# Talking-heads attention and a squared-ReLU MLP: the order of a step that has transposes and two A v pairs

## The chip, the cores and the metric

The kernel runs on one core of a Trainium2 chip. The metric is device time in microseconds, from one launch that holds everything; the time before is the median of three runs. Five queues work side by side: TensorE (matmuls and transposes, PE in the rows; its weight loads are PEld), VectorE (DVE), ScalarE (ACT), GpSimd (POOL) and SyncE (SP, which issues most transfers). In each queue the instructions stand in the order in which the program wrote them, and they wait for semaphores of the other queues.

## The reference

The inputs are q, k, v (4 batches, 12 heads, 448 positions, 64 channels), two 12 x 12 matrices that mix heads, and the weights of an MLP (768 to 2048 to 768).

```python
scores = scale * np.matmul(q, k.transpose(0, 1, 3, 2))
scores = np.einsum('bhij,hg->bgij', scores, w_pre)
scores = scores - np.max(scores, axis=-1, keepdims=True)
attn = np.exp(scores)
attn = attn / (np.sum(attn, axis=-1, keepdims=True) + 1e-09)
attn = np.einsum('bhij,hg->bgij', attn, w_post)
attn_out = np.matmul(attn, v)
x = np.ascontiguousarray(attn_out.transpose(0, 2, 1, 3)).reshape(B * S, H * D)
h = x @ w_in
r = np.maximum(h, 0.0)
return (s * (r * r) + b) @ w_out
```

Everything is float32. The kernel keeps that precision by splitting an operand into a high part (rounded) and a low part (what the rounding left) and adding three matmuls per product.

## The kernel before, in words

**Chunks, blocks, steps.** The query rows of each batch are cut into 4 chunks of 110 or 118 rows, 16 in all. A chunk is cut into 11 or 12 blocks of 9 or 10 rows; a block holds its rows for all 12 heads, so up to 120 partitions, by 448 keys. There are 180 blocks, and the attention is one loop of steps (line 851). Step s starts each block at a different stage: it transfers block s+5 out of the chunk's scores (`relayout`, SyncE), splits s+2 into high and low part (`split`, GpSimd), mixes the heads of s (`premix`, three matmuls into `pm`, L603), takes its maximum (VectorE, L605), its exponentials and their sum (ScalarE, L610, and the sum's scaling into `st`, L614, called total(s) below), normalizes s-1 (`normalize`: a reciprocal on VectorE, L622, and the half-precision high part `eh` on ScalarE, L624), forms the remainder of s-1 (VectorE, L631), mixes s-3 again with the second matrix (`postmix`, 12 matmuls into `po`, L646), and copies the result of s-4 into the chunk's tile A (`evacuate`, VectorE, L662).

**What is planned into steps.** Lines 675 to 781 make a list `plan` of work for other chunks, sorted by step and by an order within it: loads (order 0), transposes of q or k (order 1), A v pairs (order 2) and q k pairs (order 3). `prep_q` and `prep_k` transpose with TensorE into a PSUM tile of the tag `sc`, copy the high part to `Tq` or `Tk` on ScalarE (L482, L462) and append the low part to a list `later`; `low_parts` (L239) subtracts on VectorE what stands in that list. `qk_pair` calls `low_parts` and then multiplies two heads (six matmuls, L503) into a tile of the same tag `sc`, which has one buffer, and ScalarE copies them to the scores S (L513). `av_pair` multiplies A with v for two heads (16 matmuls, L531); `copy_x` copies finished sums out (ScalarE, L553).

Lines 715 to 725 take the A v pairs of a chunk two by two. Where not both of their steps follow a step with transposes, both pairs go into one step, and the transposes of the step before that one are moved into it:

```python
                    steps[i] = steps[i + 1] = steps[j]
                    for n, x in enumerate(plan):
                        if x[0] == steps[j] - 1 and x[3] in (prep_q, prep_k):
                            plan[n] = (steps[j], *x[1:])
```

That happens for 20 steps: 15, 20, 26, 45, 49, 56, 60, 65, 71, 90, 94, 101, 105, 110, 116, 135, 139, 146, 150 and 157. In 26, 71 and 116 it is k that is transposed, in the others q. Each of them also has a q k pair.

**The order within a step.** The main loop writes, for one of these steps: an instruction of the weights' conversion (`convert_step`, VectorE, only in some steps), `normalize(s-1)`, `premix(s)` with maximum and exponentials, `evacuate(s-4)`, `remainder(s-1)`, the loads, `postmix(s-3)`, and then the plan: transposes, two A v pairs, the q k pair with the low part ahead of it. So the transposes' high part is on ScalarE behind total(s), and their low part on VectorE behind the remainder.

After the attention come the two GEMMs of the MLP in two rounds over the hidden width (`gemm1_part` L254, `gemm2` L311); the first pieces of the first one are mixed into the last chunk's steps.

Of the kernel before, what the change touches and what calls it, by code (L numbers as in the profile page):

```python
# [21 lines left out]
def talking_heads_attention__then__act_relu2_kernel(  # L22
# [14 lines left out]
    B, H, S, D = q.shape  # L37
# [8 lines left out]
    NP = H // 2  # L46
# [18 lines left out]
    blocks = []  # L65
# [10 lines left out]
    NB = len(blocks)  # L76
# [112 lines left out]
    def convert_step(upto):  # L189

        if done["run"] is None:
            if done["conv"] >= min(upto, len(units)):
                return False
            done["run"] = conversion(done["conv"])
        try:
            next(done["run"])
        except StopIteration:
            done["run"] = None
            done["conv"] += 1
        return True  # L200
# [33 lines left out]
    later = []  # L234
# [7 lines left out]
    turn = {"bank": 0, "ops": 0}  # L242
# [327 lines left out]
        if ci >= NCH - 2:  # L570
            copy_x()

    blk_t, hl_t, po_t, e_t, eh_t = {}, {}, {}, {}, {}

    def relayout(t):
        ci, i0, ni = blocks[t]
# [17 lines left out]
    def premix(t):  # L594
        n = blocks[t][2] * H
        hl = hl_t.pop(t)

        tag = "px" if t % 3 == 2 else "pm"
        pm = ps.tile([P, 512], F32, tag=tag, name=f"pm_{t}", bufs=banks.count(tag))
        for _ in range(2 if t < first[1] - 1 else 1 if t < first[1] + 3 else 0):  # L600
            nc.tensor.matmul(pm, keep[:, :P], keep, start=True, stop=True)
        for m, (w, x) in enumerate(((wpre_lo, 0), (wpre_hi, 1), (wpre_hi, 0))):
            nc.tensor.matmul(pm[:n, :S], w[:n, :n], hl[:n, x, :], start=(m == 0), stop=(m == 2))  # L603
        st = smp.tile([BP, 4], F32, tag="st", name=f"st_{t}")
        nc.vector.tensor_reduce(  # L605
            out=st[:n, 0:1], in_=pm[:n, :S], axis=AX.X, op=ALU.max, negate=True
        )

        e = pm[:, :S]
        nc.scalar.activation(e[:n], e[:n], AF.Exp, bias=st[:n, 0:1], accum_out=pm[:n, S:S + 1])  # L610
        e_t[t] = (e, st)

        total = pm[:, S:S + 1]
        nc.scalar.activation(  # L614
            st[:n, 2:3], total[:n], AF.Copy, scale=2.0 ** -15, bias=1e-9 * 2.0 ** -15
        )

    def normalize(t):

        n = blocks[t][2] * H  # L620
        e, st = e_t[t]
        nc.vector.reciprocal(st[:n, 3:4], st[:n, 2:3])  # L622
        eh = blkp.tile([BP, 2, S], F16, tag="eh", name=f"eh_{t}", bufs=3)
        nc.scalar.activation(eh[:n, 0, :], e[:n], AF.Copy, scale=st[:n, 3:4])  # L624
        eh_t[t] = eh
# [10 lines left out]
    def postmix(t):  # L636
        ci, i0, ni = blocks[t]
        n = ni * H
        eh = eh_t.pop(t)
        if i0 == 0:  # L640
            a_t[ci] = ap_.tile([P, NC, H, CH], F32, tag="A", name=f"A_{ci}")
        po = ps.tile([P, 512], F32, tag="po", name=f"po_{t}", bufs=2)
        for c in range(NC):
            j0 = min(c * P, S - P)
            for m, (x, y) in enumerate(((1, 0), (0, 1), (0, 0))):
                nc.tensor.matmul(  # L646
                    po[:, c * BP:(c + 1) * BP],
                    eh[:n, x, j0:j0 + P],
                    wpost[:n, y].rearrange("p g i -> p (g i)"),
                    start=(m == 0),  # L650
                    stop=(m == 2),
                )
        po_t[t] = po
# [10 lines left out]
    LD, LS = 5, 2  # L664
    CONV0 = 12
# [7 lines left out]
    plan, load = [], {}  # L673

    def at(step, order, f, *args):
        plan.append((step, order, len(plan), f, args))
# [12 lines left out]
    for ci in range(2, NCH):  # L689
        b, _, _ = chunks[ci]  # L690
        w0 = first[ci - 1] - LD
        news = chunks[ci - 1][0] != b
        back = w0 - (first[ci - 2] - LD)
        if news:
            starts = (w0 - back + 6, w0 - back + 2)
        else:
            starts = (w0 - back + (10 if back == 12 else 8), w0 + 4)
        for half, step in enumerate(starts):
            at(step, 1, prep_q, ci, half)
            load[step] = 0.375  # L700
        if ci > 2:
            at(min(starts) - 8, 0, load_q, ci)
        for p, step in enumerate(visits(ci)):
            if news:
                t = w0 - back + 8 if p == 0 else w0 + 2 * p - 2
                at(t, 1, prep_k, b, p)
                load[t] = 0.6
                at(t - 6, 0, load_k, b, p)
            at(step, 3, qk_pair, ci, p)
            load[step] = load.get(step, 0) + QK_COST  # L710
    for ci in range(NCH):
        b = chunks[ci][0]
        w0 = first[ci + 1] + 4
        if ci < NCH - 2:
            after = visits(ci + 3) if ci + 3 < NCH else [first[NCH - 1] - LD + i for i in (1, 3, 5, 7)]
            steps = [x for x in visits(ci + 2) if x >= w0] + [x for x in after if x < first[ci + 2] + 4]
            assert len(steps) == NP
            behind = {x[0] + 1 for x in plan if x[3] in (prep_q, prep_k)}
            for i in range(0, NP, 2):
                if steps[i] not in behind or steps[i + 1] not in behind:  # L720
                    j = i if steps[i] in behind or steps[i + 1] not in behind else i + 1
                    steps[i] = steps[i + 1] = steps[j]
                    for n, x in enumerate(plan):
                        if x[0] == steps[j] - 1 and x[3] in (prep_q, prep_k):
                            plan[n] = (steps[j], *x[1:])
            for p, step in enumerate(steps):
                at(step, 2, av_pair, ci, p)
                load[step] = load.get(step, 0) + AV_COST
                if b + 1 < B and chunks[ci + 1][0] != b:
                    at(step, 4, load_v, b + 1, p)  # L730
            continue
        w1 = first[ci + 2] + 4 if ci + 2 <= NCH else NB + 100
        if ci == NCH - 1:
            w0 = NB + 4
        for p in range(NP):
            when = w0 + p * min(w1 - w0, 12) / NP
            fill.append((when, w0, w1 - 1, AV_COST, 1, av_pair, (ci, p)))
    w0 = first[NCH - 1] - XA + 2
    for i in range(NHEAD * NKC):
        if i < NHEAD * NKC - LATE:  # L740
            j = i - (NHEAD * NKC - LATE - 4)
# [9 lines left out]
    for s in range(NB + 5):  # L751
        spent = max(spent, -0.4) + load.get(s, 0)
        left, held = [], set()
        for x in fill:
            _, lo, hi, cost, order, f, args = x
# [16 lines left out]
        fill = left  # L772
        spent -= FILL
    assert not fill
    plan.sort(key=lambda x: (x[0], x[1], x[2]))
    state = {"next": 0}

# [70 lines left out]
    tail = first[NCH - 1]  # L848
    pairs = {x[0] for x in plan if x[3] is qk_pair}
    full = {s for s in pairs if s - 1 not in pairs and s <= tail - XA} | set(range(first[1] + 2))  # L850
    for s in range(NB + 4):
        if s == tail - LD:
            early.close()
            rp = ctx.enter_context(tc.tile_pool(name="rp", bufs=1, side="right", reuse_waits="tile"))
            rp.tile([P, S], F32, tag="xraw", name="place_xraw", bufs=NKC)
            for n in range(NU_EARLY, NU_EARLY + NU_TAIL):
                w_pool[n] = rp
                place_w(n)
            rp.tile([P, X_GAP // 4], F32, tag="gap", name="gap_x", bufs=1)
            rp.tile([P, 2, S], F32R, tag="x", name="place_x", bufs=NKC)  # L860
            rp.tile([P, END_GAP // 4], F32, tag="end", name="gap_end", bufs=1)
        if s + LD < NB:
            relayout(s + LD)
        if s + LS < NB:
            split(s + LS)
        if 0 <= s - 1 < NB:
            ops = 7 * NU_EARLY
            if not later and turn["ops"] < ops * (s - CONV0) / (tail - LD - 2 * NP - CONV0):
                turn["ops"] += convert_step(NU_EARLY)
            normalize(s - 1)  # L870
        if s not in full:
            if 0 <= s - 4 < NB:
                evacuate(s - 4)
            if s <= tail - XA:
                low_parts()
        if s < NB:
            premix(s)
        low_parts()
        if s in full and 0 <= s - 4 < NB:
            evacuate(s - 4)  # L880
        if s < 2:
            qk_pair(1, NP - 2 + s)
        if 0 <= s - 1 < NB:
            remainder(s - 1)
        run_plan(s, True)
        if 0 <= s - 3 < NB:
            postmix(s - 3)
        run_plan(s, False)
        if 0 <= s - (tail - LD) < NKC // 2:
            for kc in range(2):  # L890
                load_x(0, 0, 2 * (s - (tail - LD)) + kc)
        if 0 <= s - (tail - XA) < NKC:
            split_x(0, 0, s - (tail - XA))
        if 0 <= s - tail < NKC:
            load_x(0, 1, s - tail)
# [17 lines left out]
    for r in range(NR):  # L913
        u0 = 2 * r * NU
        n = NHEAD if r == 0 else NF // 2
# [91 lines left out]
```

## Time and profile before

| what | value |
|---|---|
| median of 3 runs | 945.66 us (945.46 to 945.89) |
| profiled execution | 943.67 us |
| its span, first to last instruction | 941.7 us |
| TensorE busy in the span | 906.8 us, 96% |
| VectorE, ScalarE, GpSimd busy | 654.0, 566.1, 397.8 us |
| granted TensorE clock, mean | 1.000 |

The profile is of one execution, 2 us below the median of the runs; durations are read from it, and times of the whole kernel are compared by their medians. The ends of matmuls are modelled, so a busy TensorE is not one at its peak. A wait is the idle time of an engine ahead of an instruction, put down to what came last. Idle time of an engine that nobody waits for costs nothing. The steps can be found in the trace by their first mixing matmul: step 15 begins at 50.75 us, step 45 at 126.95, step 61 at 172.43 and step 158 at 420.54; the GEMMs alone begin at about 485.

### The profile page before, as it was taken

To read this page: it belongs to the slowest core of one execution; us is meant where nothing else is said; L and a number is where in the kernel's file an instruction comes from. 1 tells how busy PE (TensorE), PEld (TensorE's weight loads), DVE (VectorE), ACT (ScalarE), POOL (GpSimd) and SP (SyncE) were. 2 spreads that over 40 slices of the span, in tenths; PEclk is the share of its full clock that TensorE was granted. 3 is DMA by queue.
4 is the path that set the end of the run, shared out by engine and by line. 5 is a ranking of instruction groups with operands and counts; after the bars stand their busy time and mean duration, and the time that the engine had idled before them with its cause. 6 is when DMAs were issued, how large, how long until landed. Compare 5 with 4: busy or idle time off the path is not lost.

```text
span 941.7 us, 19942 instructions
## 1 busy us (share of the span) xinstructions
PE 906.8 (96%) x7538; PEld 784.7 (83%) x7538; DVE 654.0 (69%) x1364; ACT 566.1 (60%) x1266; POOL 397.8 (42%) x454
## 2 busy tenths in 40 slices
PE   8989998899898998989999999999999999999998
PEld 5667776677676776767789999999999999999998
DVE  5888987889878897879789129975505934986211
ACT  5878877788777887778877877221117687700000
POOL 4866675666666676767614223100002333300000
PEclk9999999999999999999999999999999999999999
DMA  5755446463565545646424212353510430255421
GB/s 146 191 141 147 147 117 172 123 164 121 146 161 136 138 136 138 154 109 173 126 72 143 76 59 85 85 176 121 177 48 26 143 93 9 78 166 178 133 93 50
DMA packets 126555, 115.22 MB, mean 122 GB/s; under 512 B 63960, under 2 KB 122348, under 8 KB 126460
## 3 DMA queue, kind: packets, MB, share of 16 engines
q1 hardware_dynamic: 116934, 102.28, 39.0%
q10 hardware_dynamic: 9366, 11.59, 3.4%
q8 instruction: 59, 0.97, 0.4%
q14 instruction: 36, 0.29, 0.1%
q0 software_dynamic: 160, 0.09, 0.1%
HBM read 58.87 MB, written 16.52 MB: 80 GB/s over the span
## 4 chain that ended last, share of the span: by engine, by line
PE 72%; ACT 14%; DVE 9%; DMA 2%; issue 1%; POOL 1%; SPq 0%; ACTq 0%; POOLq 0%; DVEq 0%
PE po L311 25%; PE ph L254 23%; PE pm L603 6%; PE sc L503 6%; PE po L646 5%; ACT pm L610 4%; ACT eh L624 4%; PE xp L531 4%; ACT S L513 3%; DVE st L605 2%; DVE A L662 2%; DVE eh L631 1%; DMA blk<-S 1%; ACT st L614 1%; PE ph_head L254 1%
## 5 line engine op out<-in xcount | busy, mean ns | idle before, releaser
L311 PE MATMUL po<-w,g 128*128 128x384 f32 x1344 | 233.5, 336 | 0.0
L311 PEld LDWEIGHTS po<-w,g 128*128 128x128 f32 x1344 | 233.0, 188 | 0.3 <-ACT ob L318 0.3
L589 POOL TENSOR_TENSOR hl<-blk,hl 120x448 fp32r<-120x448 f32 (+1 forms) x179 | 206.2, 1152 | 14.9
L272 POOL TENSOR_TENSOR g<-h,g 128x448 fp32r<-128x448 f32 x64 | 79.5, 1243 | 279.9 <-ACT g L271 266.5
L254 PE MATMUL ph<-x,w 128*128 128x448 f32 x810 | 164.1, 362 | 0.0
L254 PEld LDWEIGHTS ph<-x,w 128*128 128x128 f32 x810 | 151.9, 188 | 10.2
L588 POOL TENSOR_SCALAR hl<-blk 120x448 fp32r<-120x448 f32 (+1 forms) x179 | 104.6, 584 | 122.2 <-PE pm L603 111.9
L646 PEld LDWEIGHTS <-eh 120*128 120x128 f16 (+1 forms) x2160 | 115.8, 98 | 44.7 <-issue 38.4
L646 PE MATMUL po<-wpost,eh 120*128 120x120 f16 (+1 forms) x2160 | 144.6, 217 | 3.8 <-DVE A L662 2.3
L631 DVE SCALAR_TENSOR_TENSOR eh<-pm,st,eh 120x448 f16<-120x448 f32 x180 | 122.1, 678 | 19.2 <-ACT eh L624 17.1
L605 DVE TENSOR_REDUCE st<-pm 120x1 f32<-120x448 f32 x180 | 110.3, 613 | 29.3 <-PE pm L603 28.6
L624 ACT ACTIVATE eh<-pm,st 120x448 f16<-120x448 f32 x180 | 114.1, 634 | 23.2 <-DVE st L622 22.6
L513 ACT ACTIVATE S<-sc 110x896 f32<-110x896 f32 (+1 forms) x91 | 83.5, 918 | 55.8 <-PE sc L503 47.8
L610 ACT ACTIVATE pm<-pm,st 120x448 f32<-120x448 f32 x180 | 109.5, 609 | 11.0 <-DVE st L605 9.9
L662 DVE COPY A<-po 128x480 f32<-128x480 f32 x168 | 107.5, 640 | 0.0
L503 PE MATMUL sc<-Tk,Tq 64*110 64x448 f32 (+1 forms) x576 | 82.5, 391 | 24.6 <-DVE Tq L239 20.6
L603 PE MATMUL pm<-hl,wpre_hi 120*120 120x448 f32 x360 | 102.2, 365 | 0.3 <-DVE hl L589 0.3
L531 PE MATMUL xp<-A,v 128*64 128x110 f32 (+1 forms) x1536 | 86.9, 263 | 0.0
L603 PE MATMUL pm<-hl,wpre_lo 120*120 120x448 f32 x180 | 82.6, 459 | 0.0
L531 PEld LDWEIGHTS xp<-A,v 128*64 128x64 f32 x1536 | 74.0, 137 | 7.2 <-issue 1.0
L503 PEld LDWEIGHTS sc<-Tk,Tq 64*110 64x110 f32 (+1 forms) x576 | 43.7, 171 | 42.5 <-DVE Tq L239 24.0
L318 ACT ACTIVATE ob<-po 128x384 f32<-128x384 f32 x28 | 13.8, 492 | 98.0 <-PE po L311 83.0
(83 smaller groups left out, 999.6 us busy)
## 6 DMA issues: line engine op xcount, KB each, us to landing
blk<-S SPq DMA_DIRECT2D x172, 210.0 KB
raw<-in_moe_w_in_dram SPq DMA_DIRECT2D x32, 384.0 KB
raw<-in_moe_w_out_dram SPq DMA_DIRECT2D x32, 384.0 KB
xraw<-xd SPq DMA_DIRECT2D x48, 224.0 KB
part<-ob ACTq DMA_DIRECT2D x28, 192.0 KB
acc<-part SPq DMA_DIRECT2D x28, 192.0 KB
out_dram<-acc ACTq DMA_DIRECT2D x28, 192.0 KB
v<-in_v_dram SPq DMA_DIRECT2D x24, 192.0 KB
```

The source lines that it names most:

```text
L254: nc.tensor.matmul(ph[:, :S], w[:, i, c0:c0 + P], x[:, y, :], start=(kc == 0 and m == 0), stop=(kc == NKC - 1 and m == 2),)
L311: nc.tensor.matmul(po[:, :NO], g[:, x, c0:c0 + P], w[:, y, :], start=(f == 0 and m == 0), stop=(f == NF - 1 and m == 2),)
L503: nc.tensor.matmul(sc[e][:n, :S], qt[r0:r0 + D, p, x, :n], kt[r0:r0 + D, y, :], start=(m == 0), stop=(m == 2),)
L531: nc.tensor.matmul(xp[e * D:(e + 1) * D, p % 4, :n], vt[:, e, c, :], a[:, c, 2 * p + e, :n], start=(c == 0), stop=(c == NC - 1),)
L589: eng.tensor_tensor(out=hl[:n, 1, :], in0=blk[:n], in1=hl[:n, 0, :].bitcast(F32), op=ALU.subtract)
L603: nc.tensor.matmul(pm[:n, :S], w[:n, :n], hl[:n, x, :], start=(m == 0), stop=(m == 2))
L605: nc.vector.tensor_reduce(out=st[:n, 0:1], in_=pm[:n, :S], axis=AX.X, op=ALU.max, negate=True)
L610: nc.scalar.activation(e[:n], e[:n], AF.Exp, bias=st[:n, 0:1], accum_out=pm[:n, S:S + 1])
L624: nc.scalar.activation(eh[:n, 0, :], e[:n], AF.Copy, scale=st[:n, 3:4])
L631: nc.vector.scalar_tensor_tensor(out=eh[:n, 1, :], in0=e[:n], scalar=st[:n, 3:4], in1=eh[:n, 0, :], op0=ALU.mult, op1=ALU.subtract,)
L646: nc.tensor.matmul(po[:, c * BP:(c + 1) * BP], eh[:n, x, j0:j0 + P], wpost[:n, y].rearrange("p g i -> p (g i)"), start=(m == 0), stop=(m = ...
L662: nc.vector.tensor_copy(dst, src)
```

## The change

In the 20 steps named above, the transposes leave the plan and are kept in a table `ahead`. There the loop issues `premix(s)` (its matmuls alone), `postmix(s-3)` and the transposes before `normalize(s-1)`; the maximum and the exponentials become a function of their own, `softmax`, which follows. The call of `low_parts` behind the maximum, which was there already, now finds the transposes' low part in the list. The conversion of weights doesn't take one of its instructions in these steps. All other steps are written as before.

```diff
@@ -601,6 +601,11 @@
         for m, (w, x) in enumerate(((wpre_lo, 0), (wpre_hi, 1), (wpre_hi, 0))):
             nc.tensor.matmul(pm[:n, :S], w[:n, :n], hl[:n, x, :], start=(m == 0), stop=(m == 2))
+        pm_t[t] = pm
+
+    def softmax(t):
+        n = blocks[t][2] * H
+        pm = pm_t.pop(t)
         st = smp.tile([BP, 4], F32, tag="st", name=f"st_{t}")
         nc.vector.tensor_reduce(
...
@@ -722,7 +728,8 @@
                     for n, x in enumerate(plan):
                         if x[0] == steps[j] - 1 and x[3] in (prep_q, prep_k):
-                            plan[n] = (steps[j], *x[1:])
+                            plan[n] = (-1, *x[1:])
+                            ahead[steps[j]] = x[3:]
...
+    plan = [x for x in plan if x[0] >= 0]
...
@@ -865,8 +873,13 @@
         if 0 <= s - 1 < NB:
             ops = 7 * NU_EARLY
-            if not later and turn["ops"] < ops * (s - CONV0) / (tail - LD - 2 * NP - CONV0):
+            if not later and s not in ahead and turn["ops"] < ops * (s - CONV0) / (tail - LD - 2 * NP - CONV0):
                 turn["ops"] += convert_step(NU_EARLY)
+            if s in ahead:
+                premix(s)
+                postmix(s - 3)
+                f, args = ahead[s]
+                f(*args)
             normalize(s - 1)
...
         if s < NB:
-            premix(s)
+            if s not in ahead:
+                premix(s)
+            softmax(s)
         low_parts()
         if s in full and 0 <= s - 4 < NB:
             evacuate(s - 4)
...
-        if 0 <= s - 3 < NB:
+        if 0 <= s - 3 < NB and s not in ahead:
             postmix(s - 3)
```

The order of TensorE's and GpSimd's instructions is the same in both kernels, but for the numbers of buffers. On ScalarE, step 45 of the kernel before reads as follows. The first row is total(44); eh_2288 is the normalized high part of block 44, pm_2290 and st_2294 belong to block 45, Tq_2032 is the high part of the transposed q, and S_2169 takes the scores of the step's q k pair.

```order
L614 ACTIVATE st_2264<-pm_2260 108x1
L624 ACTIVATE eh_2288<-pm_2260,st_2264 108x448
L610 ACTIVATE pm_2290<-pm_2290,st_2294 120x448
L614 ACTIVATE st_2294<-pm_2290 120x1
L482 ACTIVATE Tq_2032<-trq_1_2313 128x2x110
L513 ACTIVATE S_2169<-sc_2_2335 110x896
```

In the changed kernel the same place reads so (lines moved by 5, buffers are numbered anew: eh_2309 is block 44, pm_2287 block 45).

```order
L619 ACTIVATE st_2264<-pm_2260 108x1
L482 ACTIVATE Tq_2032<-trq_1_2304 128x2x110
L629 ACTIVATE eh_2309<-pm_2260,st_2264 108x448
L615 ACTIVATE pm_2287<-pm_2287,st_2311 120x448
L619 ACTIVATE st_2311<-pm_2287 120x1
L513 ACTIVATE S_2169<-sc_2_2335 110x896
```

The copy of the transposes moved ahead of the normalization of 44 and the exponentials of 45; the scores' copy keeps its place. The same holds for the other 19 steps.

On VectorE, step 49 of the kernel before shows both moves at once: the low part of Tq, and a conversion instruction (L181). st_2429 is block 48, st_2463 block 49, A_2434 takes block 45 and then 46.

```order
L181 SCALAR_TENSOR_TENSOR w_1735<-raw_712,u_1737 128x384
L622 RECIPROCAL st_2429<-st_2429 120x1
L605 TENSOR_REDUCE st_2463<-pm_2459 120x1
L662 COPY A_2434<-po_2435 128x48x10
L631 SCALAR_TENSOR_TENSOR eh_2457<-pm_2425,st_2429,eh_2457 120x448
L239 TENSOR_TENSOR Tq_2482<-trq_0_2483,Tq_2482 128x4x110
L622 RECIPROCAL st_2463<-st_2463 120x1
L662 COPY A_2434<-po_2469 128x48x10
```

In the changed kernel VectorE's queue at step 49 is this one (Tq_2470 is the same tile of q, st_2480 block 49).

```order
L627 RECIPROCAL st_2429<-st_2429 120x1
L610 TENSOR_REDUCE st_2480<-pm_2453 120x1
L239 TENSOR_TENSOR Tq_2470<-trq_0_2471,Tq_2470 128x4x110
L667 COPY A_2434<-po_2435 128x48x10
L636 SCALAR_TENSOR_TENSOR eh_2478<-pm_2425,st_2429,eh_2478 120x448
L181 SCALAR_TENSOR_TENSOR w_1735<-raw_712,u_1737 128x384
L627 RECIPROCAL st_2480<-st_2480 120x1
L667 COPY A_2434<-po_2457 128x48x10
```

The low part moved ahead of the evacuation and the remainder, as in all 20 steps; the conversion moved behind the remainder, into step 50, which happens in steps 15, 49 and 135 alone.

## Rows read from the trace of the kernel before

**Rows 1.** Windows: stretch, us, busy us (count) by engine, PEclk, DMA share, GB/s.

```profile
50.75:420.54 369.79, 344.47 (x4009) 264.58 (x4006) 313.00 (x669) 290.89 (x734) 247.60 (x291) 1.00 0.53 141
...
126.95:172.43 45.48, 39.82 (x471) 30.43 (x467) 37.44 (x81) 33.80 (x87) 29.29 (x34) 1.00 0.59 149
```

**Rows 2.** Waits of PE, 50.75 to 420.54: us in total, times, longest.

```profile
PE sc L503 <- DVE Tq L239: 19.8, 17, 1.8
PE sc L503 <- DVE Tk L239: 2.4, 4, 0.7
PE po L646 <- DVE A L662: 2.3, 7, 0.4
```

**Rows 3.** Chain that ended last, 126.95 to 137.67 (steps 45 to 48), by line.

```profile
by line: ACT pm L610 16.9%; ACT eh L624 16.8%; ACT S L513 16.1%; PE sc L503 8.3%; DVE raw L175 6.9%; DVE eh L631 6.4%; DVE A L662 5.2%; DVE st L605 5.0%; ACT st L614 4.9%; DVE Tq L239 3.7%; DVE u L179 3.4%; issue 3.3%; ACT xs L553 3.1%; DVE
```

**Rows 4.** Timeline of PE, step 45: start us, us, instruction, [idle before <-releaser].

```profile
128.85 0.36 PE L478 MATMUL trq<-ident,nq 110*128 110x110 f32 x2
129.14 1.73 PE L531 MATMUL xp<-A,v 128*64 128x110 f32 x32
132.01 0.87 PE L503 MATMUL sc<-Tk,Tq 64*110 64x448 f32 x6 [1.14 <-DVE Tq L239]
...
134.82 0.81 PE L646 MATMUL po<-wpost,eh 108*128 108x120 f16 x12
```

**Rows 5.** Timeline of ACT, step 45.

```profile
129.43 0.17 ACT L614 ACTIVATE st<-pm 108x1 f32<-108x1 f32 x1
129.89 0.63 ACT L624 ACTIVATE eh<-pm,st 108x448 f16<-108x448 f32 x1 [0.29 <-DVE st L622]
130.43 0.60 ACT L610 ACTIVATE pm<-pm,st 120x448 f32<-120x448 f32 x1
...
131.12 0.17 ACT L614 ACTIVATE st<-pm 120x1 f32<-120x1 f32 x1
131.19 0.35 ACT L482 ACTIVATE Tq<-trq 128x220 fp32r<-128x220 f32 x1
132.92 0.92 ACT L513 ACTIVATE S<-sc 110x896 f32<-110x896 f32 x1 [1.39 <-PE sc L503]
```

**Rows 6.** Timeline of DVE, step 45 and the start of 46.

```profile
129.72 0.60 DVE L605 TENSOR_REDUCE st<-pm 120x1 f32<-120x448 f32 x1
130.24 0.65 DVE L662 COPY A<-po 128x480 f32<-128x480 f32 x1
130.80 0.68 DVE L631 SCALAR_TENSOR_TENSOR eh<-pm,st,eh 108x448 f16<-108x448 f32 x1
131.57 0.39 DVE L239 TENSOR_TENSOR Tq<-trq,Tq 128x220 fp32r<-128x220 f32 x1
131.87 0.15 DVE L622 RECIPROCAL st<-st 120x1 f32<-120x1 f32 x1
131.94 0.64 DVE L662 COPY A<-po 128x480 f32<-128x480 f32 x1
133.71 0.62 DVE L605 TENSOR_REDUCE st<-pm 120x1 f32<-120x448 f32 x1 [1.14 <-PE pm L603]
```

**Rows 7.** Timeline of PE, step 41: two A v pairs and q k, no transposes.

```profile
119.65 1.73 PE L531 MATMUL xp<-A,v 128*64 128x110 f32 x32
121.31 0.85 PE L503 MATMUL sc<-Tk,Tq 64*110 64x448 f32 x6
```

**Rows 8.** Timeline of step 26, where k is transposed.

```profile
81.40 0.61 PE L458 MATMUL trk<-ident,nk 128*128 128x128 f32 x4
...
81.69 0.63 ACT L624 ACTIVATE eh<-pm,st 120x448 f16<-120x448 f32 x1 [0.29 <-DVE st L622]
```

**Rows 9.** Timeline of DVE, step 49: the conversion instruction.

```profile
139.31 0.82 DVE L181 SCALAR_TENSOR_TENSOR w<-raw,u 128x384 fp32r<-128x384 uint32 x1
```

**Rows 10.** Timeline of POOL, steps 56 and 57.

```profile
162.85 0.57 POOL L588 TENSOR_SCALAR hl<-blk 120x448 fp32r<-120x448 f32 x1 [1.84 <-PE pm L603]
```

**Rows 11.** Instructions of line L503: duration ns min/median/max, first and last start.

```profile
L503 PEldq EVENT_SEMAPHORE  x26: 51/51/51, 12.5 to 346.8; - x26
```

More of the change, by code (lines that the diff above doesn't have):

```diff
@@ L571, in av_pair @@
             copy_x()
-    blk_t, hl_t, po_t, e_t, eh_t = {}, {}, {}, {}, {}
+    blk_t, hl_t, pm_t, po_t, e_t, eh_t = {}, {}, {}, {}, {}, {}
     def relayout(t):
@@ L710, in talking_heads_attention__then__act_relu2_kernel @@
             load[step] = load.get(step, 0) + QK_COST
+    ahead = {}
     for ci in range(NCH):
```

## Prediction

> **What bounds the kernel now.** I read the table by stretches first [rows 1]. In the stretch that the change can reach, from 50.75 us (the start of step 15) to 420.54 us (the end of step 157), TensorE is busy 344.47 of 369.79 us, so 25.3 us of it are idle; VectorE is busy 313.00 and ScalarE 290.89. Of this stretch, steps 45 to 60 are the densest: 45.48 us with 39.82 of TensorE and 37.44 of VectorE. In both rows the granted clock is 1.00. The waits of TensorE in the same stretch come next [rows 2]: 19.8 us in 17 waits and 2.4 us in 4 waits stand before the q k matmuls (L503), which wait for a low part that VectorE writes (L239), and 2.3 us before the post-mixing (L646), which waits for an evacuation. That is nearly all of the idle time. 17 + 4 waits are the 20 steps with transposes and two A v pairs, and one more (a Tk wait after step 33, at most 0.7 us, the longest of its row).
>
> The chain of waits says why the low part is late [rows 3]. From one such step (45) to the next (49) the chain that ended last runs on ScalarE and VectorE: Exp (L610), normalization (L624) and the S copy (L513) lead, and TensorE's q k has 8.3%. TensorE runs ahead of these two in the short steps and is caught up by them at L503.
>
> The timelines of step 45 show the place. On TensorE the transposes start at 128.85 and last 0.36 us, the 32 A v matmuls start at 129.14 and last 1.73 (end 130.87), and q k starts at 132.01 after 1.14 us of waiting [rows 4]. On ScalarE total(44) ends at 129.60; then come eh(44) (129.89), Exp(45) (130.43) and, only at 131.19, the high part of Tq, 0.35 us [rows 5], though its transposes were done at 129.21. On VectorE max(45), A(41) and the remainder of block 44 precede the low part, which runs 131.57 to 131.96 [rows 6]. q k must wait for that, since transposes and scores share one PSUM tile (tag `sc`, one buffer). After the wait the others stand idle too: VectorE 1.14 us before max(46) [rows 6], ScalarE 1.39 us before the S copy [rows 5].
>
> **The change part by part.** No instruction is added or removed, and the order on TensorE and GpSimd is the same as before. Two queues change at 20 places: on ScalarE the high part goes ahead of eh(s-1), Exp(s) and total(s); on VectorE the low part goes ahead of A(s-4) and the remainder of s-1. At three of these steps (15, 49, 135) one conversion instruction of VectorE moves to the next step, and with one of them one weight load on SyncE's queue; SyncE keeps its order otherwise.
>
> *Step 45 anew.* ScalarE is free at 129.60, after the transposes: high part 129.60 to 129.95. VectorE ends max(45) at 130.32: low part 130.32 to 130.71. The A v matmuls end at 130.87, so q k waits for nothing and 1.14 us go. Margin: 0.16 us. What is put behind is later than before: eh(44) starts at 129.95 (+0.06), Exp(45) at 130.58 (it has to wait for eh, +0.15), A(41) at 130.66 (+0.42), the remainder of 44 at 131.25 (+0.45), to 131.93.
>
> *Who waits for these.* The S copy needs total(45), about 131.44 (Exp's start plus the 0.86 us from 130.43 to 131.29 that Exp and total took [rows 5]), and q k, which now ends at about 131.67: TensorE is still last, by 0.2 us. The next maximum needs premix(46), which ends some 1.7 us after q k's start, as 132.01 to 133.71 shows [rows 4, 6], so at 132.57. VectorE has to do recip(45) and A(42) between 131.93 and then, which took from 131.87 to 132.58 before: 0.71 us, done by 132.64. So VectorE's 1.14 us of idle time are used up and it is about 0.1 us late. Postmix(44), the first reader of the remainder of 44, stood at 134.82 [rows 4] and will stand near 133.6: the margin is 1.7 us. From the S copy on, all three engines are where they were, 1.1 to 1.2 us earlier.
>
> *The other 19.* I worked them out in the same way from their rows, which repeat these. In 18 of the 20 the low part lands before the A v matmuls end, by 0.1 to 0.5 us; steps 15 and 49 keep 0.3 and 0.1 us of wait. The three steps with Tk (26, 71, 116) have transposes that end later than ScalarE is free: in step 26 they run 81.40 to 82.01, and eh(25), at 81.69 before, comes after the high part at 82.60, 0.91 us later [rows 8]. There q k waited least and the margins are the widest.
>
> *The sum.* Waits before L503: 22.2 us, less at most 0.7 for step 33: 21.5 [rows 2]. Plus the overlap that an unbroken stream has: in step 41, with two pairs and no transposes, A v ends at 121.38 and q k starts at 121.31 [rows 7], 0.07 us times 20, 1.4. Less the 0.4 that steps 15 and 49 keep. Less the semaphores: since the low part no longer stands behind A(s-4) and the remainder, 13 mixings get a wait instruction of their own on TensorE's queue; the nearest row is 0.051 us each [rows 11], so 0 to 0.7, and I take 0.7. Less the three conversions: each is up to 0.82 us [rows 9] that falls after the low part, into the step in which VectorE has no idle time any more. Bounds: a gain of 0.5 in all (the ahead step's maximum comes earlier) to a loss of 2.5; I take 0.5, since the two-pair step that follows gives VectorE time to catch up. 21.5 + 1.4 - 0.4 - 0.7 - 0.5 = 21.3 us.
>
> *Against the run.* The profiled execution took 943.67 us (span 941.7), so 922.4 for a like one; the median of the runs shown is 945.66, 2.0 above it, and it is medians that are compared: 945.66 - 21.3 = 924.4 us.
>
> *Covers.* GpSimd's split and the transfers before it have to keep pace. In the dense stretch GpSimd, right after a split whose block had come late, stands idle for 1.84 us until TensorE frees a buffer [rows 10]. If the transfers came not a bit earlier, steps 49 and 56 would take 2.5 us from that margin and TensorE would lose about 0.7 there. SyncE's issues mostly wait for GpSimd, so they shift too; I take nothing.
>
> [...]
>
> **The rivals.**
>
> *The two-engine chain is the real bound.* Between the 20 steps the chain runs on ScalarE and VectorE [rows 3]; in the dense stretch VectorE has 37.44 us of work [rows 1], and taking 1.1 to 1.5 us from each of four steps leaves some 40.3 us, so it would be 93% busy. The margins of 0.1 to 0.5 us are thin: a chain that is 0.7 us longer per period than I worked out leaves a stall of 0.2 to 0.6, so about 0.4 times 20, 8 us. Then 924.4 + 8 = 932.4. Against it: the moved copies leave that chain (eh, Exp and total no longer stand before them), and VectorE's 1.14 us are idle now.
>
> *The wait only changes its place.* Post-mixing now waits openly for A(s-4), which comes 0.42 us later, and mixing for the remainder; if TensorE lost there what it wins at L503, the time would stay at 945.7. For it: the 2.3 us that stand there already [rows 2]. Against it: postmix(43) follows premix(46), so at 132.3 at the earliest, and A(41) ends at 131.30.
>
> *The head of ScalarE's queue.* The high part waits for transposes that stand behind pre- and post-mixing, and eh and Exp can't pass it. If that held them until the remainder missed its reader, TensorE would stall two steps later. It decides from a delay of 1.7 us (step 45's margin), and the kernel gets slower from 2.8 us (margin plus gain): at 3.0 us each step loses 0.2, 945.66 + 4 = 950 us. Against it: the longest delay of eh is 0.9 us [rows 8], and in 45 it is 0.06.
> [...]
>
> **How the numbers follow.** Forecast 0.82, the chain 0.13, no change 0.03, slower 0.02. About 0.2% (1.9 us) is what a measurement of this kernel can tell from no change, so faster 0.95, same 0.03, slower 0.02. The forecast's own range: at best the 0.4, 0.7 and 0.5 aren't lost and the 2.3 us before L646 go as well, a gain of 25.2 (920.5); at worst the conversions cost 2.5 and the transfers 0.7, a gain of 18.6 (927.1). From there it reaches to the chain's case: 921 to 931.
>
> **What would show it.** L503's wait for L239 inside the 20 steps falls from 22 us to under 1; step 45 gets 1.1 to 1.2 us shorter; ScalarE's high part starts within 0.1 us of total(s-1) or of the transposes; VectorE's 1.1 us of idle time before the next maximum vanishes; waits before L646 stay near 2.3 us. I am wrong if L503 still waits for the low part (the chain), if L646 or the mixing wait by as much more, or if what is gained by 420 us is not there at the end: there TensorE has to be without gaps from the first GEMM on.

## The result: 924.82 us, 0.9776 of the time before

The changed kernel takes 924.82 us (median of 6 runs, 923.66 to 925.39); the kernel before took 945.83 (6 runs on the same chip, 945.46 to 946.66). The ratio is 0.9776, with a 95% interval of 0.9763 to 0.9788: 21.0 us less, where 21.3 were forecast. The profiled execution took 925.39 us (span 923.7) with a granted clock of 0.999; beside the profile of before (943.67) that is 18.3 less, so the two profiles are 2.7 us closer together than the medians. In the rounds of the experiments, on three chips, 33 executions of the kernel before have their granted TensorE clock on record: the 15 at 0.999 or 1.000 took 942.8 to 944.3 us, the 18 at 0.996 to 0.998 took 944.9 to 947.0; the changed kernel's six ran at 0.999 or 1.000.

### The profile page after: what moved, and what is told of

It is laid out like the page before. It is cut to its first block, busy times and chain, and to the rows that moved or that the text cites. A ratio compares the mean times of both kernels' runs of the same rounds, so it can differ in the third digit from the quotient of the medians.

```text
span 923.7 us, 19935 instructions
## 1 busy us (share of the span) xinstructions
PE 907.8 (98%) x7538; PEld 785.2 (85%) x7538; DVE 651.6 (71%) x1364; ACT 566.1 (61%) x1266; POOL 398.0 (43%) x454
## 4 chain that ended last, share of the span: by engine, by line
PE 83%; ACT 6%; DVE 5%; DMA 3%; POOL 1%; issue 1%; SPq 0%; ACTq 0%; POOLq 0%
PE po L311 25%; PE ph L254 24%; PE pm L603 9%; PE po L651 8%; PE xp L531 7%; PE sc L503 6%; DMA blk<-S 2%; ACT S L513 2%; ACT pm L615 2%; DVE A L667 1%; DVE st L610 1%; PE ph_head L254 1%; ACT eh L629 1%; PE trk L458 1%; PE trq L478 1%; ACT xs L553 1%
## 5 line engine op out<-in xcount | busy, mean ns | idle before, releaser
L603 PE MATMUL pm<-hl,wpre_hi 120*120 120x448 f32 x360 | 102.6, 366 | 1.2 <-POOL hl L589 0.9
L503 PE MATMUL sc<-Tk,Tq 64*110 64x448 f32 (+1 forms) x576 | 82.5, 391 | 3.0 <-DVE Tq L239 0.7
L603 PE MATMUL pm<-hl,wpre_lo 120*120 120x448 f32 x180 | 82.6, 459 | 0.0
L603 PEld LDWEIGHTS pm<-hl,wpre_hi 120*120 120x120 f32 x360 | 64.7, 182 | 7.8 <-POOL hl L589 2.7
```

The costliest lines, as they stand in the source:

```text
L503: nc.tensor.matmul(sc[e][:n, :S], qt[r0:r0 + D, p, x, :n], kt[r0:r0 + D, y, :], start=(m == 0), stop=(m == 2),)
```

## The profile after

The stretch of [rows 1] now runs from 51.62 (step 15) to 401.79 us (the end of step 157), and steps 45 to 60 from 125.32 to 165.59. Columns as in [rows 1].

```profile
51.62:401.79 350.17, 344.37 (x4009) 264.66 (x4006) 310.35 (x668) 290.59 (x734) 247.71 (x291) 1.00 0.56 149
125.32:165.59 40.27, 39.53 (x470) 30.44 (x467) 35.81 (x79) 33.78 (x87) 27.43 (x32) 1.00 0.62 155
```

The stretch is 19.6 us shorter with the same 344.4 us of TensorE: what went is idle time, 25.3 us before and 5.8 now. Steps 45 to 60 went from 45.48 to 40.27 us, about 1.3 for each of the four steps. The waits of TensorE there, which answer to [rows 2] (lines from 605 on stand 5 further down: 646 is now 651, 662 is 667; in e9 to e11, below, lines from 398 on stand one further still):

```profile
PE po L651 <- DVE A L667: 2.6, 8, 0.5
PE pm L603 <- POOL hl L589: 0.9, 3, 0.5
PE trk L458 <- ACT S L513: 0.8, 1, 0.8
PE sc L503 <- DVE Tk L239: 0.6, 1, 0.6
```

The 19.8 us before the q k matmuls (L503) are gone altogether; the 0.6 left is the Tk wait after step 33, not one of the 20 steps. The wait for the evacuation is what it was (2.3 before, 2.6 now). Two rows are new, for GpSimd's split (0.9) and for an S copy (0.8). The chain from one dense step to the next (125.32 to 134.84), by line, answers to [rows 3]:

```profile
by line: PE po L651 27.0%; PE pm L603 23.7%; PE xp L531 17.4%; PE sc L503 16.6%; DVE raw L175 7.9%; DVE A L667 5.9%; PE trq L478 2.1%; DVE st L627 0.8%; issue 0.4%
```

Exp, normalization and S copy led it before; now the four largest shares are TensorE's, 84.7% together, and the conversion (L175) and the evacuation that it delays come next. Step 45 on TensorE, ScalarE and VectorE, as in [rows 4 to 6]; each row is start us, us, instruction, and in brackets the idle time before it with its releaser:

```profile
126.61 0.79 PE L651 MATMUL po<-wpost,eh 120*128 120x120 f16 x12 [0.45 <-DVE A L667]
127.24 0.36 PE L478 MATMUL trq<-ident,nq 110*128 110x110 f32 x2
127.53 1.73 PE L531 MATMUL xp<-A,v 128*64 128x110 f32 x32
129.18 0.87 PE L503 MATMUL sc<-Tk,Tq 64*110 64x448 f32 x6
129.98 0.47 PE L603 MATMUL pm<-hl,wpre_lo 120*120 120x448 f32 x1
```

```profile
127.82 0.17 ACT L619 ACTIVATE st<-pm 108x1 f32<-108x1 f32 x1
127.89 0.35 ACT L482 ACTIVATE Tq<-trq 128x220 fp32r<-128x220 f32 x1
128.22 0.64 ACT L629 ACTIVATE eh<-pm,st 108x448 f16<-108x448 f32 x1
128.75 0.60 ACT L615 ACTIVATE pm<-pm,st 120x448 f32<-120x448 f32 x1
...
130.09 0.92 ACT L513 ACTIVATE S<-sc 110x896 f32<-110x896 f32 x1 [0.47 <-PE sc L503]
```

```profile
125.09 0.83 DVE L175 SCALAR_TENSOR_TENSOR raw<-raw 128x384 uint32<-128x384 uint32 x1
...
125.92 0.63 DVE L667 COPY A<-po 128x480 f32<-128x480 f32 x1
...
128.10 0.61 DVE L610 TENSOR_REDUCE st<-pm 120x1 f32<-120x448 f32 x1
128.63 0.38 DVE L239 TENSOR_TENSOR Tq<-trq,Tq 128x220 fp32r<-128x220 f32 x1
128.92 0.65 DVE L667 COPY A<-po 128x480 f32<-128x480 f32 x1
...
130.89 0.62 DVE L610 TENSOR_REDUCE st<-pm 120x1 f32<-120x448 f32 x1
```

The high part of Tq starts as total(44) ends, 0.29 us after the transposes (127.60); the low part starts right behind the maximum and ends at 129.01, 0.25 before the A v matmuls end (129.26; 0.16 was worked out). q k starts without a wait and overlaps A v by 0.07. No idle time of VectorE is printed before max(46) any more, and the S copy waits 0.47 us instead of 1.39. Postmixing waits 0.45 at 126.61, for an evacuation (125.92 to 126.55) that stood behind the conversion at 125.09: the wait that a later experiment removes.

**Where the time went, step by step.** Measured from each step's first mixing matmul to the next one's, the 20 steps add up to 110.26 us before and 88.09 after: 22.2 less. Step 45 went from 5.86 to 4.66, step 15 from 6.11 to 4.29, step 26 from 4.95 to 4.34. In all 20, q k now starts 0.07 us before A v ends, with the low part written 0.20 to 0.84 us earlier. Against that, a few steps that the change doesn't touch got longer: 30 (+1.04), 62 (+0.74), 63 (+0.45), 156 (+0.28) and 170 (+0.16), 2.7 us in all. What they wait for, on GpSimd in steps 60 and 61, and on ScalarE and TensorE in step 30:

```profile
166.92 0.57 POOL L588 TENSOR_SCALAR hl<-blk 120x448 fp32r<-120x448 f32 x1 [4.08 <-DMA blk<-S]
```

```profile
90.81 0.92 ACT L513 ACTIVATE S<-sc 110x896 f32<-110x896 f32 x1 [2.06 <-DMA blk<-S]
```

```profile
91.78 0.66 PE L458 MATMUL trk<-ident,nk 128*128 128x128 f32 x4 [0.83 <-ACT S L513]
```

All three go back to the transfer of a block (`blk`): GpSimd waits 4.08 us for it, ScalarE 2.06 before it may write the scores S, and the transposes wait for that copy. SyncE, which issues it, is shown from 154 to 173 us (SPq is its queue; a row can stand for several issues in a line, waits between them included):

```profile
155.81 2.87 SPq L447 DMA_DIRECT2D nq<-in_q_dram  x2
158.77 0.40 SPq L398 DMA_DIRECT2D v<-in_v_dram  x1
159.26 0.67 SPq L401 DMA_DIRECT2D v<-in_v_dram  x1
160.01 0.54 SPq L398 DMA_DIRECT2D v<-in_v_dram  x1
160.65 1.47 SPq L401 DMA_DIRECT2D v<-in_v_dram  x1
162.21 0.55 SPq L558 DMA_DIRECT2D xd<-xs  x1
162.84 10.27 SPq L580 DMA_DIRECT2D blk<-S  x8
```

From 155.8 to 162.1 us it issues q and v loads one after the other (the first q load waits up to 157.26 for TensorE), and the eight block transfers come behind them. This cover was taken at nothing in the sum.

## The experiments

All are edits of the changed kernel; times are medians, ratios are to the kernel before, run on the same chip in the same rounds.

| experiment | us | ratio [95% interval] |
|---|---|---|
| changed kernel | 924.82 | 0.9776 [0.9763, 0.9788] |
| e1 high part alone | 938.52 | 0.9937 [0.9922, 0.9952] |
| e2 low part alone | 943.97 | 1.0002 [0.9992, 1.0011] |
| e3 transposes a step earlier | 927.32 | 0.9818 [0.9803, 0.9832] |
| e4 conversions stay in the 20 steps | 924.88 | 0.9789 [0.9773, 0.9805] |
| e5 low part formed twice | 929.97 | 0.9839 [0.9822, 0.9856] |
| e6 no conversion in the step before either | 921.61 | 0.9748 [0.9734, 0.9761] |
| e7 last v loads six steps later | 927.16 | 0.9817 [0.9796, 0.9839] |
| e8 both | 924.65 | 0.9777 [0.9762, 0.9792] |
| e9 v loads on GpSimd's queue | 926.52 | 0.9802 [0.9788, 0.9817] |
| e10 the same on e6 | 923.56 | 0.9770 [0.9756, 0.9784] |
| e11 v loads on ScalarE's queue, on e6 | 940.47 | 0.9931 [0.9906, 0.9957] |

**Which half of the change does it?** In e1 the high part stays ahead on ScalarE, and the low part goes back behind evacuation and remainder on VectorE:

```diff
             softmax(s)
-        low_parts()
+        if s not in ahead:
+            low_parts()
         if s in full and 0 <= s - 4 < NB:
```

> The changed kernel with VectorE's old order in the 20 steps: the low part comes behind the remainder again, the high part stays ahead of eh on ScalarE. TensorE's and ScalarE's orders are those of the changed kernel. My theory (q k waits for the low part, and both copies must be early): in step 45 the remainder ends at about 131.5 as before and the low part at 131.8 instead of 131.96, so 0.1 to 0.2 us per step come back, 2 to 4 us in all: 942 to 944 us. Rival (the chain runs on ScalarE, so that moving its copy is what counts): 924 to 928 us.

In e2 ScalarE has its old order (the transposes' copy behind total(s)), and only the low part moves:

```diff
                 premix(s)
                 postmix(s - 3)
+            normalize(s - 1)
+            if s in ahead:
+                softmax(s)
                 f, args = ahead[s]
                 f(*args)
-            normalize(s - 1)
```

> The changed kernel with ScalarE's old order in the 20 steps: the high part comes behind total(s) again; VectorE takes the low part right behind the maximum, as in the changed kernel. My theory: the low part can't begin before the high part, at about 131.57 in step 45, VectorE waits for it with the evacuation and the remainder behind it, q k starts as late as in the kernel before, and both of these come about 1.3 us later, which the step's end hides only in part: 946 to 952 us. Rival (the low part's place alone counts): 924 to 930 us.

e1 gained 5 to 6 us (6.0 by the ratio, 5.1 in the 20 steps), more than the 2 to 4 that were expected; e2 gained nothing, but lost nothing either. TensorE's waits, in 50 to 420 us of e1 first and in 50 to 422 of e2 below:

```profile
PE sc L503 <- DVE Tq L239: 14.2, 17, 1.0
```

```profile
PE sc L503 <- DVE Tq L239: 18.8, 17, 1.4
```

Both leave most of the wait standing, so neither half alone brings as much as a third of the gain: the two moves need each other. VectorE's timeline in step 45 of e2 shows why the early place is worth nothing without the early copy:

```profile
131.59 0.39 DVE L239 TENSOR_TENSOR Tq<-trq,Tq 128x220 fp32r<-128x220 f32 x1 [1.25 <-ACT Tq L482]
131.89 0.65 DVE L667 COPY A<-po 128x480 f32<-128x480 f32 x1
...
133.73 0.62 DVE L610 TENSOR_REDUCE st<-pm 120x1 f32<-120x448 f32 x1
```

The low part waits 1.25 us at the head of VectorE's queue for ScalarE's copy, with evacuation and remainder standing idle behind it, and starts at 131.59 against 131.57 before [rows 6]. That the kernel isn't slower for it was the miss of the expectation: VectorE had 1.14 us of idle time before max(46), and the late work fits into it (no idle time is printed before 133.73). In the 20 steps e1 is 5.1 us shorter than before: the steps that transpose two pairs of heads got 0.16 to 0.21 shorter, those with four pairs 0.35 to 0.41, and steps 15 and 49 0.96 and 0.88, which includes their conversion; the three with k got 0.10 to 0.20 longer.

**Does the place of the transposes matter?** e3 leaves them in the step before the two A v pairs, so the PSUM tile is free a step earlier and no low part can be late:

```diff
-                            plan[n] = (-1, *x[1:])
-                            ahead[steps[j]] = x[3:]
+                            pass
```

> The transposes stay in the step before the two A v pairs, and nothing is issued ahead. By the program's order ScalarE and VectorE are exactly as in the changed kernel; only TensorE differs: the 20 transposes come before premix(s) instead of behind postmix(s-3). My theory: the low part is early, so the wait before q k stays away, but the transposes now meet the scores' PSUM tile (one buffer) while ScalarE still copies it out, which ends 0.3 to 0.6 us after TensorE gets there in the 17 steps with q: 929 to 934 us. Rival (only the order on ScalarE and VectorE counts): 924 to 926 us.

The gain shrank by about 4 us, a little less than expected. The wait only moves: in 50 to 402 us the transposes now wait for the scores' copy of the step before, since they share its tile.

```profile
PE trq L478 <- ACT S L513: 4.2, 12, 0.5
```

**How much room is left on VectorE?** e5 forms every one of the 20 low parts twice, the same values again:

```diff
             softmax(s)
+        if s in ahead:
+            later.extend(list(later))
         low_parts()
```

> The changed kernel, but VectorE forms the low part twice in the 20 steps, one right behind the other, into the same place. This measures the margin. A second one adds 0.31 us (two heads) to 0.54 us (four heads, or k). My theory: 0.1 to 0.5 us of it fit before the A v matmuls end, so q k waits for 0 to 0.2 us, about 2 to 5 us in all: 927 to 930 us. Rival (VectorE and ScalarE bound the time between these steps): nearly all of 20 times 0.43 shows, 8 us: 932 to 934 us.

```profile
PE sc L503 <- DVE Tq L239: 5.0, 15, 0.6
```

It costs 6.0 us by the ratios, between the two expectations and nearer to the theory's upper end. The wait for the low part is back, 0.3 us at a time: in step 45 the two take 0.80 us on VectorE where one took 0.38, which is more than the margin of 0.25. So the low part now arrives just in time: 0.4 us more of VectorE's work in one of these steps already costs 0.3.

**What do the conversions cost?** e4 lets them stand in the 20 steps again, and e6 keeps them out of the step before as well:

```diff
-            if not later and s not in ahead and turn["ops"] < ops * (...):
+            if not later and turn["ops"] < ops * (...):                                        # e4
+            if not later and s not in ahead and s + 1 not in ahead and turn["ops"] < ops * (...):  # e6
```

(`(...)` stands for the rest of the condition, which is the same in all three.)

> The changed kernel, but a conversion instruction may be taken in the 20 steps as before; that puts it back at the head of VectorE's queue in steps 15, 49 and 135. My theory: there it delays the maximum and with it the low part by up to 0.8 us, while the step behind it has less to do: 0 to 1.5 us slower than the changed kernel, 925 to 926.3 us. Rival (the conversions cost less at the old place, as I priced their move at 0.5 us): 924.3 us.

> The changed kernel, but the conversion of weights takes no instruction in the step before the 20 either. The waits before the second mixing (2.6 us in the changed kernel's trace, 8 times) stand where such an instruction holds up the evacuation. My theory: 1.5 to 2.5 us go, 922.3 to 923.3 us. Rival (the instruction holds up another step just as much): 924.5 to 925.5 us.

e4 can't be told from the changed kernel (the 20 steps add up to the same within 0.1 us), so that part of the change is worth nothing here. e6 is the best kernel of all: 0.9748, its interval wholly below the changed kernel's, and by the ratios 2.6 us better, where 1.5 to 2.5 were expected. Its waits in 50 to 402 us:

```profile
PE pm L603 <- POOL hl L589: 0.9, 3, 0.6
...
PE po L651 <- DVE A L667: 0.4, 2, 0.2
```

The wait for the evacuation went from 2.6 to 0.4 us, as expected; step 45 takes 4.05 us, 0.61 less than in the changed kernel and 1.81 less than before. The 20 steps together are 3.8 us shorter (eight of them by 0.3 to 0.6 each), and 1.1 come back in other steps, the largest in 59, 108 and 149 (0.3 to 0.4 each).

**Do the transfers cause the losses in 62 and 63?** e7 puts the last two of each batch's v loads six steps later, e8 does so on top of e6:

```diff
-                    at(step, 4, load_v, b + 1, p)
+                    at(step + (6 if p > 3 else 0), 4, load_v, b + 1, p)
```

> The changed kernel, but the last two loads of v for the next batch are issued six steps later, so that they aren't on SyncE's queue ahead of the blocks' transfers for steps 60 to 63. In the changed kernel's trace steps 62 and 63 are 1.2 us longer than before, behind a block that GpSimd waited 4.1 us for. My theory: these 1.2 us come back, and 0.3 at step 156: 923.3 to 924 us. Rival (the transfers are late for another reason, or it moves to another step): 924.5 to 925.5 us.

> The two before in one kernel. My theory: the gains add, 921 to 922.5 us. Rival: no better than the better of the two.

Steps 62, 63 and 156 got back what they had lost (1.32, 2.23 and 1.32 us, within 0.01 of before), and still e7 was slower than the changed kernel, by more than the rival had allowed for. The delay came up elsewhere: step 75 went from 1.71 to 2.90 us and step 120 from 1.72 to 3.65. TensorE's new wait in 50 to 402 us, and ScalarE in step 120, both of e7:

```profile
PE trk L458 <- ACT S L513: 3.4, 3, 1.7
```

```profile
311.80 0.92 ACT L513 ACTIVATE S<-sc 110x896 f32<-110x896 f32 x1 [2.95 <-DMA blk<-S]
```

The S copy may write only when the block transfers have read the old scores, and these stand behind the later v loads: the two transfers that SyncE issues at 306.00 and 306.97 us in the changed kernel come at 307.91 and 308.88 in e7. With e6 the same happens (4.4 us in two such waits), and e8's rival was right: at 924.65 us it is no better than e6 alone (921.61), nor than the changed kernel. Part of the two medians is the clock: e7's executions took 925.9 and 926.9 us at a granted clock of 0.999 and 1.000, and 927.2 to 931.7 at 0.996 to 0.998.

This points at SyncE's queue, which has no room wherever the loads stand in it. e9 takes the 36 v issues of batches 1 to 3 off it, onto GpSimd's; e10 does that on top of e6, and e11 puts them on ScalarE's queue, also on e6:

```diff
+        queue = nc.sync if b == 0 else nc.gpsimd      # e11: nc.scalar
-        nc.sync.dma_start(
+        queue.dma_start(
             t[:, :, :NC - 1, :], src[:, :KM, :].rearrange("h (p c) d -> p h c d", c=NC - 1)
         )
-        nc.sync.dma_start(t[P - KL:, :, NC - 1, :], src[:, KM:, :].rearrange("h p d -> p h d"))
+        queue.dma_start(t[P - KL:, :, NC - 1, :], src[:, KM:, :].rearrange("h p d -> p h d"))
```

> The changed kernel with the v loads of batches 1 to 3 (36 issues, four in a step with two A v pairs) on GpSimd's queue in place of SyncE's; nothing else moves. Theory (SyncE's queue): the 3.3 us of v issues that stand ahead of block 62's transfer at 158.77 to 162.11 are gone, steps 62, 63 and 156 get back 0.74 + 0.45 + 0.28, step 30 keeps its loss (its transfers stand behind k loads): 923.3 to 923.6 at a before of 945.83, ratio 0.9762 to 0.9766. Unlike in the kernel with later v loads, nothing gets longer at steps 75 and 120. Rival (the transfers' own time on the DMA engines counts, not the queue they are issued from): 924.8, steps 62 and 63 unchanged. Second rival (GpSimd has no room): four issues at the 0.6 us of its first loads are 2.4 us beside a split of 1.74 in a step of 4.4; at SyncE's 0.8 they would be 3.3 and a split would come 0.6 late in nine steps: up to 929, with waits of the mixing for L589.

> The same on top of the kernel that keeps conversions out of the 20 steps and out of the steps before them (921.61 on its chip, ratio 0.9748). Theory: another 1.2 to 1.5 us less, 920.1 to 920.4 (ratio 0.9733 to 0.9736). Rival (transfers' own time): 921.6. Second rival (GpSimd has no room): up to 926.

> The same 36 issues on ScalarE's queue, on top of the kernel that keeps conversions clear. ScalarE has about 3 us of work in a two-pair step of 4.4 us. Theory: an issue costs ScalarE what it costs SyncE (0.5 and 1.0 us), 3.3 us in nine steps, of which some 1.4 is free: up to 1.9 us lost in each, so 930 to 939 with SyncE's gain lost in it. Rival: an issue costs ScalarE 0.35 us, as those of its results in the GEMMs do (1.4 us in a step, all of it free): 920.1 to 921.

SyncE in e9; compare 162.84 in the changed kernel:

```profile
157.74 14.17 SPq L581 DMA_DIRECT2D blk<-S  x8
```

The block transfers start 5 us earlier, and steps 62, 63 and 156 take 1.32, 2.23 and 1.32 us, without a loss at 75 or 120. The same bytes still move, so it was their place in SyncE's queue and not the transfers themselves: the theory held for 62 and 63. It missed step 30, which was to keep its loss and takes 1.73 us here. In the whole it fell, since GpSimd has no room either (the second rival):

```profile
154.87 0.77 POOL L399 DMA_DIRECT2D v<-in_v_dram  x1
155.63 0.62 POOL L402 DMA_DIRECT2D v<-in_v_dram  x1
156.25 0.73 POOL L399 DMA_DIRECT2D v<-in_v_dram  x1
156.97 0.61 POOL L402 DMA_DIRECT2D v<-in_v_dram  x1
```

Four issues take 2.71 us of GpSimd, and its splits come late. In e10 six steps near the v loads (56, 60, 101, 105, 146, 150) are 0.45 to 0.47 us longer than in e6, 2.8 in all, more than the 1.8 that steps 62, 63 and 108 got back. In step 56 it is the mixing that waits for the split's low part:

```profile
150.92 0.66 PE L604 MATMUL pm<-hl,wpre_hi 120*120 120x448 f32 x2 [0.20 <-POOL hl L590]
```

(The weight load ahead of it waited 0.48 us for the same; the printed 0.20 is against the modelled end of the matmul before.) In e9 steps 56, 101, 146 and 150 are 0.39 to 0.57 us longer than in the changed kernel, and steps 59 and 104, which wait for an evacuation, 0.92 each. In e11 the same issues stand between two steps' work on ScalarE; near 150 us, and then TensorE's waits for a remainder in 50 to 422:

```profile
148.64 0.37 ACTq L399 DMA_DIRECT2D v<-in_v_dram  x1
149.05 0.68 ACTq L402 DMA_DIRECT2D v<-in_v_dram  x1
149.77 0.89 ACTq L399 DMA_DIRECT2D v<-in_v_dram  x1
150.70 0.60 ACTq L402 DMA_DIRECT2D v<-in_v_dram  x1
151.35 0.81 ACT L554 ACTIVATE xs<-xp,xscale 128x400 f32<-128x400 f32 x2 [1.81 <-DMA v<-in_v_dram]
```

```profile
PE pm L604 <- DVE eh L637: 11.5, 9, 2.5
```

The sums' copy stands 1.81 us idle behind the four issues, the normalization and the remainder stand behind that, and the mixing waits for them nine times, as many as there are steps with such loads. By its ratio the time is 939.3 us, the upper end of what was expected, but that expectation left out the clock. In five stretches of e11's profile the granted clock is 0.50, where [rows 1] have 1.00; the first follows the wait of 1.82 us at 153.54. The columns of the first row are those of [rows 1]; the second is a post-mixing in that stretch, 1.38 us where the one at 150.13 took 0.80:

```profile
153.70:157.00 3.30, 3.30 (x18) 2.41 (x17) 3.27 (x7) 3.19 (x7) 1.71 (x2) 0.50 0.62 161
```

```profile
154.78 1.38 PE L652 MATMUL po<-wpost,eh 120*128 120x120 f16 x12
```

The runs of e11 spread with it, from 934.55 us at a mean clock of 0.998 to 943.76 at 0.991. So the waits for the remainder are what it shows; how much of the size is theirs and how much the clock's is not separated.

## Why the prediction was right, and which term was not

- **The waits, 21.5 us, and the overlap, 1.4.** Right. No wait before q k is left in the 20 steps, and all of them have the overlap of 0.07 us. e1 and e2 show that this needs both moves. Alone I mis-sized them: e2 lost nothing because I had given no worth to VectorE's idle time, and e1 gained some 2 us more than I had worked out from step 45, since the steps with four pairs of heads and steps 15 and 49 gain more than step 45 does.
- **Steps 15 and 49 keep 0.4 us.** Wrong: they keep nothing, and the low part lands 0.37 and 0.54 us early there. The three steps with Tk, said to have the widest margins, have 0.42.
- **13 more waits on TensorE's queue, 0.7 us.** The 13 are there (122 event semaphores at L603 against 109). 21.5 + 1.4 - 0.7 = 22.2 is what the 20 steps gave, but no run takes the semaphores away by themselves, so their price isn't shown.
- **The conversions, 0.5 us.** The moved ones cost nothing that can be measured (e4). Those in the step before do (2.6 us by e6): they are behind the wait at L646 that the prediction left where it was, rightly for this change, without saying that it could be had.
- **Covers, taken at nothing, at most 0.7.** The mis-sized term: "SyncE's issues mostly wait for GpSimd, so they shift too; I take nothing." They don't all shift. In steps 49 to 62 q and v loads fill SyncE's queue, and blocks came up to 4.1 us late for GpSimd. Steps 30, 62, 63 and 156 lost 2.5 us. For 62 and 63 the queue is shown to be the cause by e7 and e9. For 156 it is not, since it is back at 1.32 us in e4 and e6 too, which move no transfer. Nor is it for step 30: it takes 1.7 to 1.8 us in before, e1, e2, e3, e5, e8 and e9, and 2.1 to 4.3 in the changed kernel, e4, e6, e7, e10 and e11, though none of these edits moves a transfer near it; what makes the difference in these two steps stays open.
- **The sum.** The profiles give -22.2 (the 20 steps), +2.7 (other steps), +0.9 (step 0 starts later, 21.41 against 20.53) and +0.6 (after the last step): -18.0 of span. Some of the last two is scatter: step 0, which no edit touches, starts between 20.39 and 21.42 us in the thirteen traces. The medians give -21.0. The terms that lost too much (0.4 and 0.5) and the one that was missed (2.5) don't cancel, so by like profiles the forecast is 3 us too good; by the medians, which it was made for, it is 0.3.
- **The step from profile to median, 2.0 us, and luck.** The forecast put these 2.0 us on the changed kernel as well, and it doesn't have them: its profiled execution (925.39) is the slowest of its six. The record says what they go with: the kernel before takes 943.5 us on average where its clock was 0.999 or 1.000, as in the profile, and 945.5 at 0.998; the six executions compared here (945.46 to 946.66) lie where the second kind does, though their own clock isn't on record. So about 2 of the 21.0 us go with a clock that the sum knows nothing of, and they made up for most of what it promised too much. That the forecast hit the median to 0.4 us is luck in that part; whether the change itself keeps the clock up isn't shown.
- **The rivals.** The chain of ScalarE and VectorE did not take over, but the low part has only 0.20 to 0.84 us to spare in each step, near the 0.1 to 0.5 that rival started from, and e5 shows that using it up costs time. The wait did not move to L646 (2.6 us). The head of ScalarE's queue cost nothing, though the copy did wait there: in step 45 the transposes were done 0.29 us before it could start, but in steps 26, 65, 71 and 116 it stood idle for 0.52 to 0.65 us, with the normalization behind it. That is far from the 1.7 us from which the rival was to decide. Step 26:

```profile
79.99 0.54 ACT L462 ACTIVATE Tk<-trk 128x448 fp32r<-128x448 f32 x1 [0.65 <-PE trk L458]
```

In e11 nothing passed the four issues on ScalarE either (1.81 us idle), and in e2 nothing passed the low part on VectorE (1.25 us).

## What to carry to other kernels

When an engine waits for the end of a chain over two others, move the whole chain ahead, not one link: the first link alone gave 5 to 6 of 21 us, the last alone nothing. Then ask of each queue that has to keep pace, the one that issues transfers too, how long it works without a gap in the densest stretch; a later place (e7, 0.9817) or another queue (e9, 0.9802) for the same loads moved the loss and didn't remove it (0.9776 for the changed kernel). And look at what stands on the critical engine one step ahead: a deferrable 0.8 us conversion there cost 0.3 to 0.6 us in each of eight steps (e6), and nothing measurable in the step itself (e4). Last, compare executions of the same granted clock before a gain is put down to a change.

## What the runs showed of the hardware

- Issuing took time on each queue that issued. A block transfer takes SyncE 0.8 us (median 0.82 in the changed kernel), the two pairs of v loads above 1.07 and 2.01 (0.40 and 0.67, 0.54 and 1.47, waits included). On GpSimd the four issues of a step took 0.77, 0.62, 0.73 and 0.61 us, on ScalarE 0.37, 0.68, 0.89 and 0.60, and a store of the GEMMs' results (`part<-ob`, 192 KB) takes ScalarE only 0.33. I had expected ScalarE to be either as dear as SyncE or as cheap as its stores; its four v loads took 2.54 us, those above on SyncE 3.08.
- Of the kernels that issue the same q, k, v and block transfers, only the faster ones showed SyncE's lack of room: steps 62 and 63 take 1.32 us and 2.22 to 2.27 in before, e1, e2 and e5, all at about 930 us or more, and 1.62 to 2.19 and 2.65 to 2.70 in e3, e4, e6 and the changed kernel (921.6 to 927.3 us).
- The granted clock fell behind waits of TensorE: in e11's profile (the first time behind 1.82 us), and once in e8's (from 312.31 us on, where a wait of 2.20 us ended at 311.82), it is 0.50 for a stretch, and in e11's first a post-mixing takes 1.38 us, 1.7 times the 0.80 of one before it. Not each wait was followed by that: before q k in step 15 of the kernel before TensorE waited 1.75 us, and its profile has a mean granted clock of 1.000.
